# Half the Fourier rows from mirrored sums through DRAM, and a bank of the Fourier stage for every third MLP group

## The chip, the core and the metric

The kernel runs on one core of a Trainium2 chip. The core has a matrix engine (TensorE, "PE" in the profile, with "PEld" for its weight loads), a vector engine ("DVE"), a scalar engine ("ACT"), a general engine ("POOL") and a queue engine ("SP") that only issues transfers. Transfers go through 16 DMA engines, which the queues of SP, ACT and POOL share. The metric is the device time of one execution in microseconds; the lower the better. The kernel before takes 309.03 us, the median of 3 runs (308.47 to 309.29).

## The reference

Two parts run after each other. The first is attention by chunks: 4 batches, 8 heads, 768 positions of 64 elements. Chunks of 32 queries look at 16 positions to the left, their own 32, 8 to the right and 8 memory positions. The heads' outputs side by side give `x` of 4 x 768 x 512. The second part is a Fourier mixing layer with an MLP:

```python
X = np.fft.fft(x, axis=1)
X = np.fft.fft(X, axis=2)
mixed = np.real(X).astype(np.float32)
u = x + mixed
mu = np.mean(u, axis=-1, keepdims=True)
var = np.mean((u - mu) ** 2, axis=-1, keepdims=True)
un = (u - mu) / np.sqrt(var + 1e-06)
ch = np.maximum(un @ w_ch1, 0.0) @ w_ch2
return u + ch
```

Because `x` is real, `mixed[s, d]` equals `mixed[(768 - s) % 768, (512 - d) % 512]`: the rows 385 to 767 of `mixed` are the rows 383 to 1 with their columns mirrored.

## The kernel before

**Who sets the order.** Every piece of work is put on a list with `plan.add(engine, cost, emit, after, take, give, ...)`. `Plan.order` (line 62) plays the list through with these costs and returns one order of pieces; the kernel issues them in that order, and each engine executes its own part strictly in it. `take` and `give` are the buffers that a piece holds; a piece is placed when the plan believes its buffers free. Pieces marked `filler` (the MLP's matmuls) have the lowest rank on PE and are placed where nothing else is ready. Between engines the hardware waits on semaphores, whatever the plan believed.

**Stages of a batch.** Attention (`attention`, line 692) runs by pairs of heads, four pairs `n` a batch: loads of q and k on POOL's queue and of v on SP's (`e_load_v`, line 289, seven transfers for each pair), turns, scores, exponentials, values, and `e_norm` (line 376), which writes `xsb`, a tile of 128 partitions x 6 row tiles x 512. The Fourier stage (`first_fourier` for batch 0, `fourier` for the others) folds `xsb` on DVE, transforms along the sequence on PE (`e_rows`, line 433, into PSUM tiles `ps`), copies the result as two fp16 parts (`up`), reverses it for the upper half (`e_dn`, line 459), and transforms along the columns: `e_columns` (line 537) makes, for each of six row tiles `kt`, a PSUM tile `pm` with 8 matmuls of 128 columns of weights and 256 moving elements. `e_sum` adds `pm` to `xsb`, `e_stats` takes mean and variance, `e_un` subtracts the mean and casts, and `e_flip` (line 572) transposes the row tile with a transfer on SP, for batches 1 to 3; batch 0 does that on PE with `tp` tiles. The MLP of a batch (`mlp`, line 903) has two halves `sh` of three row tiles each: 16 groups `e_ch1` of four matmuls into `ph`, each followed by a relu on ACT (`e_relu`), then three row tiles `e_ch2` of 16 matmuls into `pc`, each followed by `e_osb` on DVE and a store `e_out` on ACT's queue.

**Banks of PSUM.** The tag "acc" has two banks for `ps` and `pm`, the tag "mlp" two for `ph`, `pc`, `tp`. Which one the MLP takes is said by

```python
def mtag(b, i):
    return "acc" if b == B - 1 and i % 3 == 2 else "mlp"
```

so only in the last batch does every third `ph` and `pc` go into an "acc" bank. The groups of `e_ch2` stand in a chain (`c2`, `mlp_prev`), so no later MLP group is placed before an earlier `e_ch2`.

**Transfers.** SP and ACT each issue their transfers in order. In the built program every transfer of these two queues takes the next of eight completion semaphores, in turn over both queues; it is issued only when the earlier transfer on that semaphore has completed. A transfer of one queue can thus wait for one of the other.

Of the kernel before, what the change touches and what calls it, by code (L numbers as in the profile page):

```python
# [10 lines left out]
FP32 = mybir.dt.float32  # L11
BF16 = mybir.dt.bfloat16
FP16 = mybir.dt.float16
AFT = mybir.ActivationFunctionType
ALU = mybir.AluOpType
# [16 lines left out]
def strided(src, off, dims):  # L32
    return bass.AP(tensor=src.tensor, offset=src.offset + off,
                   ap=[list(src.ap[0])] + [list(d) for d in dims])
# [105 lines left out]
def kernel(  # L140
# [11 lines left out]
    nc = tc.nc  # L152
    B, H, S, D = q.shape
    DM = out.shape[2]
# [35 lines left out]
    seq = [(b, pr) for b in range(B) for pr in (0, 2, 1, 3)]  # L190

    plan = Plan(dict(qs=NS, ks=NS, va=NV, kTb=NKT, qT=2, tr=1, sc=1, xa=1, e1=3,
                     xsb=3, fold=2, hl=1, up=4, dn=4, acc=2, mlp=2, un=6, unT=2, hT=1, osb=3))
    add = plan.add
    MLPS = 1000000

# [189 lines left out]
            xa[:, :, :, 0:D], zs.unsqueeze(3).to_broadcast([P, 3, 2, D]), ALU.mult)  # L386


    zy_of, pq_of, ff_of, hl_of, ps_of, up_of, pm_of, un_of, tp_of = ({} for _ in range(9))
    mu_of, unT_of, rstd_of, g_of = {}, {}, {}, {}  # L390
    mid = cpool.tile([P, 2, NST, 1], FP16)
    mid32 = cpool.tile([P, NST, 1], FP32)
    warm = cpool.tile([P, 1], FP32)
    gate = cpool.tile([P, 1], FP32)

    def e_zy(b, par, c):
# [60 lines left out]
                                up[:, 0].rearrange("p k s -> p s k"), ALU.subtract)  # L457

    def e_dn(b, par, ab):
        dn = fpool.tile([P, 2, HS], FP16, tag="dn", bufs=4, name="dn")  # L460
        nc.vector.tensor_copy(dn, rev_ap(up_of[b, par, ab][2], HS, HS, [[2 * NK, 2]]))
        up_of[b, par, ab][1] = dn

    def g_zy(par, g):
        if g == 0:
# [82 lines left out]

    def e_sum(b, kt):
        uv = xs[b][:, kt, :].rearrange("p (j c) -> p c j", c=2)  # L550
        nc.vector.tensor_tensor(uv, pm_of.pop((b, kt)), uv, ALU.add)  # L551

    def e_stats(b, kt):
        if kt == 0:
# [17 lines left out]
    def e_flip(b, kt):  # L572
        if kt == 0:
            unT_of[b] = fpool.tile([P, NDT, S], FP16, tag="unT", bufs=2, name="unT")
        nc.sync.dma_start_transpose(unT_of[b][:, :, ts(kt, P)], un_of.pop((b, kt)))

    def e_unT(b, kt):
        if kt == 0:
# [6 lines left out]
        nc.gpsimd.tensor_tensor(rstd, rstd, mhalf, ALU.pow)  # L585


    def mtag(b, i):
        return "acc" if b == B - 1 and i % 3 == 2 else "mlp"

    ph_of, pc_of, hT_of, osb_of = ({} for _ in range(4))

# [18 lines left out]
                             start=(ht == 0), stop=(ht == NHT - 1))  # L611

    def e_osb(b, sh, stl):
        st = sh * 3 + stl
        osb_of[b, st] = osb = fpool.tile([P, DM], FP32, tag="osb", bufs=3, name="osb")
        nc.vector.scalar_tensor_tensor(osb, pc_of.pop((b, sh, stl)), rstd_of[b][:, st:st + 1],  # L616
                                       xs[b][:, st, :], ALU.mult, ALU.add)

    def e_out(b, st):
        nc.scalar.dma_start(out[b, ts(st, P), :], osb_of.pop((b, st)))  # L620


    t_zero = add("DVE", 0.2, e_zero, rank=-21)
    t_table = add("ACT", 1.4, lambda: nc.scalar.activation(warm, zero, AFT.Sin), [t_zero], rank=-3)
# [169 lines left out]
    def first_fourier():  # L794
# [37 lines left out]
                                              give=(tag,))  # L832
        return columns_of(0, t_rest)

    def fourier(b):
        nrm = [[t_norm[b * HP + i, g] for i in ii for g in range(2)] for ii in ((0, 1), (2, 3))]
        t_rest = {}
        zy = {}
        ff = hi = None
        for par in range(2):  # L840
            zy[par] = [None]
            for c in range(2):
                zy[par].append(add("DVE", 0.96, lambda par=par, c=c: e_zy(b, par, c),
                                   nrm[c] + [ff, zy[par][-1]],
                                   take=("fold",) if c == 0 else ()))
            pq = add("DVE", 1.86, lambda par=par: e_pq(b, par), zy[par], take=("fold",),
                     give=("fold",))
            prev = pq
            for ab in range(2):
                ff = add("DVE", 1.1, lambda par=par, ab=ab: e_ff(b, par, ab), [pq, prev],  # L850
                         take=("fold",) if ab == 0 else (), give=("fold",) if ab == 1 else ())
                prev = ff
                hi = add("ACT", 0.85, lambda par=par, ab=ab: e_hi(b, par, ab), [ff, hi],
                         take=("hl",) if ab == 0 else ())
                lo = add("DVE", 0.96, lambda par=par, ab=ab: e_lo(b, par, ab), [hi],
                         give=("fold",) if ab == 1 else ())
                rw = add("PE", 1.95 if par == 0 and ab == 1 else 1.0,
                         lambda par=par, ab=ab: e_rows(b, par, ab), [lo, t_sines],
                         take=("acc",), give=("hl",) if ab == 1 else ())
                up = add("ACT", 0.6, lambda par=par, ab=ab: e_up(b, par, ab), [rw], take=("up",))  # L860
                t_rest[par, ab] = add("DVE", 0.6, lambda par=par, ab=ab: e_rest(b, par, ab),
                                      [up], give=("acc",))
        return columns_of(b, t_rest)

    def columns_of(b, t_rest):
        t_dn = {}
        for par in range(2):
            for ab in range(2):
                t_dn[par, ab] = add("DVE", 0.36, lambda par=par, ab=ab: e_dn(b, par, ab),
                                    [t_rest[par, ab]], take=("dn",))  # L870
        t_un = {}
        allr = list(t_rest.values())
        cols = {}

        def columns(kt):
            cols[kt] = add("PE", 0.9, lambda: e_columns(b, kt),
                           allr + [t_rows] + (list(t_dn.values()) if kt > 2 else []),
                           take=("acc",), rank=len(plan.tasks) + (15 if kt == 3 else 0),
                           give=("up",) * 4 if kt == 2 else ("dn",) * 4 if kt == 5 else ())

        sa = None
        columns(0)
        for kt in range(NST):
            if kt + 1 < NST:
                columns(kt + 1)
            su = add("DVE", 0.7, lambda kt=kt: e_sum(b, kt), [cols[kt]], give=("acc",))
            sa = add("DVE", 0.9, lambda kt=kt: e_stats(b, kt), [su, sa])
            un = add("ACT", 0.72, lambda kt=kt: e_un(b, kt), [sa], take=("un",))
            if b > 0:
                t_un[kt] = add("SP", 0.1, lambda kt=kt: e_flip(b, kt), [un, t_un.get(kt - 1)],  # L890
                               take=("unT",) if kt == 0 else (), give=("un",), moved=0.8,
                               loose=True)
                continue
            tp = add("PE", 0.26, lambda kt=kt: e_turn_u(b, kt), [un, t_idh], take=("mlp",),
                     give=("un",))
            t_un[kt] = add("DVE", 0.43, lambda kt=kt: e_unT(b, kt), [tp, t_un.get(kt - 1)],
                           take=("unT",) if kt == 0 else (), give=("mlp",))
        rs = add("POOL", 1.0, lambda: e_rstd(b), [sa])
        return t_un, rs
# [3 lines left out]
    def mlp(b, t_un, rs):  # L903
        for sh in range(2):
            relu = []
            c2 = None
            for ht in range(NHT):
                ph = add("PE", 0.65, lambda sh=sh, ht=ht: e_ch1(b, sh, ht),
                         mlp_prev + [t_un[3 * sh + i] for i in range(3)] + t_w1,
                         take=(mtag(b, ht),), give=("unT",) if sh == 1 and ht == NHT - 1 else (),  # L910
                         rank=MLPS + len(plan.tasks), filler=True)
                relu.append(add("ACT", 0.5, lambda sh=sh, ht=ht: e_relu(b, sh, ht),
                                [ph, relu[-1] if relu else None],
                                take=("hT",) if ht == 0 else (), give=(mtag(b, ht),),
                                rank=RELU(len(plan.tasks))))
            for stl in range(3):
                st = 3 * sh + stl
                for part in range(4):
                    end = part == 3
                    c2 = add("PE", 0.88, lambda sh=sh, stl=stl, part=part: e_ch2(b, sh, stl, part),  # L920
                             [relu[4 * part + 3], t_w2[part], c2], take=(mtag(b, stl),) if part == 0 else (),
                             give=("hT",) if stl == 2 and end else (),
                             rank=MLPS + len(plan.tasks), filler=True)
                os_ = add("DVE", 0.76, lambda sh=sh, stl=stl: e_osb(b, sh, stl), [c2, rs],
                          take=("osb",), 
                          give=(mtag(b, stl), "xsb") if st == NST - 1 else (mtag(b, stl),),
                          rank=RELU(len(plan.tasks)))
                mlp_prev[0] = c2
                add("ACT", 0.1, lambda st=st: e_out(b, st), [os_], give=("osb",), moved=0.9,
                    rank=RELU(len(plan.tasks)))  # L930

# [46 lines left out]
```

## Time and profile before

| | |
|---|---|
| median of 3 runs | 309.03 us (308.47 to 309.29) |
| the profiled execution | 308.85 us, of which 307.1 us are the span from first to last instruction |
| PE | 289.5 us busy (94%), 3148 matmuls |
| `ph` matmuls, L596 | 512, 91.6 us |
| `pc` matmuls, L610 | 384, 86.9 us |
| `pm` matmuls, L545 | 192, four groups of 48 with 9.2 us each |
| DVE, ACT, POOL | 171.2, 161.5, 40.8 us busy |
| DMA | 28.93 MB, mean 94 GB/s |

The profile is of one execution. A line "L545" is a line of the kernel; `out<-in` are tile names. Busy times of matmuls overlap, since they are pipelined, so their pace is better read from the chain of work that ended last, which is followed back from the last instruction, or from start to start in the order of time. Waits name the engine, the line and what ended the wait. Rows "SPq" are the queue's own: how long it stood at a transfer before issuing it, or took to issue it. The lines shown below are word for word from the profile and the answers of the trace.

### The profile page before, as it was taken

Reading aid. Unit: us, or ns where it says so; the run is one execution under the profiler, and the core shown is the slowest. Engines: PE = TensorE matmul, PEld = TensorE weight load, DVE = VectorE, ACT = ScalarE, POOL = GpSimd, SP = SyncE. Lnnn points to the kernel's source line nnn. Section 1 sums busy time; section 2 is a strip of 40 time slices with the busy share of each in tenths; the row PEclk is TensorE's granted clock in tenths of the full one; section 3 lists DMA queues with packets and bytes.
Section 4 is the critical chain, followed back from the end, with each engine's and each line's share of the span. In section 5 each row is a group of like instructions: output and inputs, shape, how many; then the busy total and the mean of one; then the engine's idle time right before and its main releaser. Section 6 shows DMA issues by size and latency. Waiting matters only on the chain.

```text
span 307.1 us, 7496 instructions
## 1 busy us (share of the span) xinstructions
PE 289.5 (94%) x3148; PEld 181.5 (59%) x3148; DVE 171.2 (56%) x371; ACT 161.5 (53%) x291; POOL 40.8 (13%) x78
## 2 busy tenths in 40 slices
PE   1399999999999999999989999999999999999994
PEld 1267678866666676666756646675554554554541
DVE  7877895975397887797764399476101001001001
ACT  6656373689884666885257423743360450531710
POOL 8806421132201102000020000000200000000000
PEclk9999999999999999999999999999999999999999
DMA  6989999999944925821361011004201101001011
GB/s 114 197 171 167 204 205 196 198 204 178 193 72 91 203 45 111 136 47 40 89 137 36 2 46 59 0 19 102 86 2 40 64 2 68 34 2 71 31 36 68
DMA packets 60289, 28.93 MB, mean 94 GB/s; under 512 B 48480, under 2 KB 56672, under 8 KB 60256
## 3 DMA queue, kind: packets, MB, share of 16 engines
q1 hardware_dynamic: 47168, 11.61, 21.0%
q0 software_dynamic: 9344, 10.49, 20.8%
q10 hardware_dynamic: 3744, 6.36, 5.7%
q8 instruction: 25, 0.41, 0.5%
q14 instruction: 8, 0.07, 0.1%
HBM read 30.28 MB, written 6.29 MB: 119 GB/s over the span
## 4 chain that ended last, share of the span: by engine, by line
PE 91%; DMA 2%; POOL 2%; DVE 1%; ACT 1%; issue 1%; POOLq 0%; ACTq 0%
PE ph L596 28%; PE pc L610 27%; PE xa L372 9%; PE pm L545 7%; PE ps L440 5%; PE idle L654 5%; PE ps L534 4%; PE sc L351 3%; DMA qs<-in_q_dram 2%; PE trk L313 2%; PE trq L313 2%; DVE osb L616 1%; POOL qs L286 0%; ACT hT L603 0%; PE tp L570 0%
## 5 line engine op out<-in xcount | busy, mean ns | idle before, releaser
L603 ACT ACTIVATE hT<-ph 128x384 f16<-128x384 f32 x128 | 60.9, 492 | 63.0 <-PE ph L596 51.5
L596 PE MATMUL ph<-unT,w_sb 128*128 128x384 f16 x512 | 91.6, 326 | 2.2 <-ACT hT L603 1.1
L610 PE MATMUL pc<-w_sb,hT 128*128 128x512 f16 x384 | 86.9, 379 | 0.0
L596 PEld LDWEIGHTS <-w_sb 128*128 128x128 f16 x512 | 47.8, 97 | 36.8 <-issue 5.7
L616 DVE SCALAR_TENSOR_TENSOR osb<-pc,rstd,xsb 128x512 f32<-128x512 f32 x24 | 18.0, 749 | 82.5 <-PE pc L610 82.4
L610 PEld LDWEIGHTS <-hT 128*128 128x128 f16 x384 | 36.8, 98 | 41.2 <-issue 0.2
L359 ACT ACTIVATE e<-sc,mbias 128x384 f32<-128x384 f32 x64 | 33.8, 583 | 13.8 <-PE sc L351 11.3
L372 PEld LDWEIGHTS xa<-va,e 128*64 128x64 f32 x768 | 25.0, 137 | 7.8 <-issue 7.0
L372 PE MATMUL xa<-va,e 128*64 128x65 f32 x768 | 29.3, 226 | 0.0
L563 ACT ACTIVATE un<-xsb,mu_s 128x512 f16<-128x512 f32 x24 | 17.2, 720 | 14.9 <-DVE mu_s L558 14.8
L382 DVE RECIPROCAL zs<-xa 128x6 f32<-128x6 f32 x32 | 6.1, 191 | 25.6 <-PE xa L372 25.5
L452 ACT CAST up<-ps 128x386 f16<-128x386 f32 x16 | 9.7, 603 | 19.1 <-PE ps L440 13.5
L551 DVE TENSOR_TENSOR xsb<-pm,xsb 128x512 f32<-128x512 f32 x24 | 16.0, 675 | 4.4 <-PE pm L545 4.2
L383 DVE TENSOR_TENSOR xsb<-xa,zs 128x384 f32<-128x384 f32 x32 | 17.8, 557 | 1.1
L557 DVE BATCH_NORM_STATS2 st<-xsb 128x6 f32<-128x512 f32 x24 | 16.4, 684 | 0.5
L654 PE MATMUL idle<-dz 128*128 128x384 bf16 x71 | 15.3, 350 | 1.0 <-DVE zero L230 1.0
L322 ACT COPY qT<-trq 128x768 bf16<-128x768 bf16 x16 | 12.8, 798 | 5.6 <-PE trq L313 5.5
L286 POOL DMA_DIRECT2D ks<-in_k_dram x16 | 10.2, 635 | 35.0 <-PE trk L313 31.4
L584 POOL TENSOR_SCALAR rstd<-mu_s 128x6 f32<-128x6 f32 x4 | 1.0, 245 | 102.0 <-DVE osb L616 57.7
L313 PE MATMUL trq<-ident_b,qs 96*64 96x96 bf16 x256 | 9.4, 221 | 5.1 <-DMA qs<-in_q_dram 5.1
L286 POOL DMA_DIRECT2D qs<-in_q_dram x16 | 10.5, 659 | 25.2 <-PE trq L313 21.5
L456 DVE TENSOR_TENSOR up<-ps,up 128x386 f16<-128x386 f32 x16 | 9.6, 598 | 7.5 <-ACT up L452 7.5
(126 smaller groups left out, 343.5 us busy)
## 6 DMA issues: line engine op xcount, KB each, us to landing
va<-in_v_dram SPq DMA_DIRECT2D x32, 220.0 KB
out_dram<-osb ACTq DMA_DIRECT2D x24, 256.0 KB
w_sb<-in_moe_w_ch_dram POOLq DMA_DIRECT2D x8, 512.0 KB, 16.9
qs<-in_q_dram POOLq DMA_DIRECT2D x16, 192.0 KB, 5.7
ks<-in_k_dram POOLq DMA_DIRECT2D x16, 192.0 KB, 6.1
va<-in_mem_v_dram SPq DMA_DIRECT2D x32, 24.0 KB
va<-in_v_dram SPq DMA_DIRECT2D x32, 22.0 KB
va<-in_v_dram SPq DMA_DIRECT2D x16, 32.0 KB
```

The costliest lines, as they stand in the source:

```text
L286: nc.gpsimd.dma_start(dst[n % NS][0:QP], src[b, 2 * pr:2 * pr + 2].rearrange("h (p j) d -> p h (j d)", j=RB))
L313: nc.tensor.transpose(out_[64 * hh:64 * hh + 64, j * w:(j + 1) * w], src[:, hh, j * D:(j + 1) * D], eye)
L359: nc.scalar.activation(e1[:, :, :, ts(half, 32)], sc[:, :, 0:6, ts(half, 32)], AFT.Exp, bias=mbias[:, half:half + 1], scale=1.0 / math.sqr ...
L372: nc.tensor.matmul(xa[64 * half:64 * half + 64, st, hh, 0:65], e1[:, hh, t6, :], v1[:, hh, 6 * g + t6, 0:65], start=True, stop=True)
L383: nc.vector.tensor_tensor(xs[b][:, 3 * g:3 * g + 3, 2 * pr * D:(2 * pr + 2) * D] .rearrange("p s (h d) -> p s h d", h=2), xa[:, :, :, 0:D] ...
L545: nc.tensor.matmul(pm[:, par, :], lhs, rhs[:, par, :], start=(im == 0), stop=(im == 3))
L563: nc.scalar.activation(un, xs[b][:, kt, :], AFT.Identity, bias=mu_of[b][:, kt, 0:1], scale=-1.0)
L596: nc.tensor.matmul(ph[:, 0:384], w1_sb[:, dt, ts(ht, P)], unT_of[b][:, dt, sh * 384:(sh + 1) * 384], start=(dt == 0), stop=(dt == NDT - 1))
L603: nc.scalar.activation(hT_of[b, sh][:, ht, :], ph_of.pop((b, sh, ht))[:, 0:384], AFT.Relu, bias=0.0, scale=-1.0)
L610: nc.tensor.matmul(pc_of[b, sh, stl], hT_of[b, sh][:, ht, ts(stl, P)], w2_sb[:, ht, :], start=(ht == 0), stop=(ht == NHT - 1))
L616: nc.vector.scalar_tensor_tensor(osb, pc_of.pop((b, sh, stl)), rstd_of[b][:, st:st + 1], xs[b][:, st, :], ALU.mult, ALU.add)
L654: nc.tensor.matmul(fill_of[0][:, 0:384], dz, strided(dz, 0, [[0, 3], [1, P]]), start=True, stop=True)
```

## The change

Two things change. First, in batches 1 to 3 `e_columns` makes only the row tiles 0, 1 and 2, the rows 0 to 383. The other three are gained from the same PSUM tiles: `e_back` writes the three upper row tiles of `xsb` to a DRAM tensor with their rows backwards inside blocks of 64, `e_mirror` reads them back into `xr` so that partition p of tile t holds row 768 - (128 t + p), and `e_sum_back` adds `pm`, read with its columns backwards, to `xr` and writes the sum into the upper half of `xsb`. Row 384, which has no mirror image, is made by `e_last_row` in row 0 of the first `pm`, after `e_sum` has read it. A `pm` bank is therefore held until `e_sum_back` has read it. The row tiles of these batches are worked on in the order 0, 3, 1 ... (`kts`, `SLOT`), and the outputs of the mirrored ones go to a second DRAM tensor (`e_out_rows`, on SP) and from there backwards to the output (`e_out_back`, on SP). `dn`, needed for batch 0 alone, becomes one buffer, which `xr` shares. Second, `mtag` gives the "acc" bank to every third MLP group in all batches.

In the built program SP issues 42 transfers more, nine of `e_back`, twelve each of `e_mirror` and `e_out_back` and nine of `e_out_rows`, and ACT nine stores less. The first `e_back` stands between the loads of v for pairs 11 and 12, its `e_mirror` between the loads for pairs 12 and 13; those of batch 2 stand behind the last load. Before `e_back` of batch 1, load 11 stands on the semaphore of batch 0's store of row tile 2. The third `e_mirror` transfer of batch 3 stands on that of batch 1's store of row tile 1.

```diff
     def e_dn(b, par, ab):
-        dn = fpool.tile([P, 2, HS], FP16, tag="dn", bufs=4, name="dn")
+        if b not in dn_of:
+            dn_of[b] = fpool.tile([P, 4, 2, HS], FP16, tag="dn", bufs=1, name="dn")
+        dn = dn_of[b][:, 2 * par + ab]
...
+    xd = nc.dram_tensor("x_rows", [2, 3, P, DM], FP32).ap()
+    od = nc.dram_tensor("out_rows", [2, 3, P, DM], FP32).ap()
...
+    def e_back(b):
+        for t in range(3):
+            r0 = xd[b % 2, t, 63:64, :]
+            nc.sync.dma_start(bass.AP(tensor=r0.tensor, offset=r0.offset,
+                                      ap=[[64 * DM, 2], [-DM, 64], [1, DM]]), xs[b][:, 5 - t, :])
+
+    def e_mirror(b):
+        xr_of[b] = xr = fpool.tile([P, 3, DM], FP32, tag="dn", bufs=1, name="xr")
+        xb = xd[b % 2].rearrange("t p d -> p t d")
+        nc.sync.dma_start(xr[1:65], xb[64:128])
+        nc.sync.dma_start(xr[65:128], xb[0:63])
+        nc.sync.dma_start(xr[0:1, 1:3], xb[63:64, 0:2])
+        nc.sync.dma_start(xr[0:1, 0:1], xb[63:64, 2:3])
+
+    def e_last_row(b):
+        pm = pm_of[b, 0]
+        for par in range(2):
+            todo = [(up_of[b, par, ab][0][:, part, HS:HS + 1], (cosD, nsinD)[ab])
+                    for ab in range(2 - par) for part in range(2)]
+            for i, (lhs, rhs) in enumerate(todo):
+                nc.tensor.matmul(pm[0:1, par, :], lhs, rhs[:, par, :], start=(i == 0),
+                                 stop=(i == len(todo) - 1))
+
+    def e_sum_back(b, kt):
+        pm, xr = pm_of.pop((b, kt)), xr_of[b]
+        y = xs[b][:, 3 + kt, :].rearrange("p (j c) -> p c j", c=2)
+        r = xr[:, kt, :].rearrange("p (j c) -> p c j", c=2)
+        nc.vector.tensor_tensor(y[:, :, 1:HD], strided(pm, HD - 1, [[HD - 1, 2], [-1, HD - 1]]),
+                                r[:, :, 1:HD], ALU.add)
+        nc.vector.tensor_tensor(y[:, :, 0], strided(pm, 0, [[2 * HD - 1, 2]]), r[:, :, 0],
+                                ALU.add)
...
+    SLOT = (0, 3, 4, 5, 1, 2)
...
     def mtag(b, i):
-        return "acc" if b == B - 1 and i % 3 == 2 else "mlp"
+        return "acc" if i % 3 == 2 else "mlp"
...
+    def e_out_rows(b, st):
+        nc.sync.dma_start(od[b % 2, st - 3], osb_of.pop((b, st)))
+
+    def e_out_back(b, st):
+        t = st - 3
+        p0 = 1 if t == 0 else 0
+        src, r0 = od[b % 2, t, p0:P, :], S - P * t - p0
+        top = out[b, r0:r0 + 1, :] if r0 < S else out[b, 0:1, :]
+        half = [[1, HD]]
+        nc.sync.dma_start(bass.AP(tensor=top.tensor, offset=top.offset,
+                                  ap=[[HD, 2], [-DM, P - p0]] + half),
+                          bass.AP(tensor=src.tensor, offset=src.offset,
+                                  ap=[[HD, 2], [DM, P - p0]] + half))
+        if p0:
+            nc.sync.dma_start(out[b, HS:HS + 1, :], od[b % 2, 0, 0:1, :])
...
     def fourier(b):
+        t_x1 = add("SP", 0.4, lambda: e_back(b), [t_norm[b * HP + i, 1] for i in range(HP)],
+                   moved=2.0, loose=True)
+        t_xr[b] = add("SP", 0.4, lambda: e_mirror(b), [t_x1], take=("dn",), moved=2.0, loose=True)
...
+        else:
+            kts = (0, 1, 3, 4, 2, 5)
...
+            if b > 0 and kt > 2:
+                if kt == 3:
+                    cols[kt] = add("PE", 0.7, lambda: e_last_row(b), [t_sum[0]])
+                return
...
+            if b == 0 or kt < 3:
+                su = add("DVE", 0.7, lambda kt=kt: e_sum(b, kt), [cols[kt]],
+                         give=("acc",) if b == 0 else ())
+                t_sum[kt] = su
+                if b > 0 and kt == 0:
+                    columns(3)
+            else:
+                su = add("DVE", 0.8, lambda kt=kt: e_sum_back(b, kt - 3),
+                         [cols.get(kt), t_sum[kt - 3], t_xr[b]],
+                         give=("acc", "dn") if kt == 5 else ("acc",))
...
+                if b and st > 2:
+                    o1 = add("SP", 0.1, lambda st=st: e_out_rows(b, st), [os_], give=("osb",),
+                             moved=0.9, loose=True)
+                    add("SP", 0.1, lambda st=st: e_out_back(b, st), [o1], moved=0.9, loose=True)
+                    continue
```

## The prediction

> **What bounds the kernel now.** I read the page's busy shares, its 40 slices, the chain that ended last, then the shapes, stretches, waits and order of time where the change acts.
>
> ```profile
> PE 289.5 (94%) x3148; PEld 181.5 (59%) x3148; DVE 171.2 (56%) x371; ACT 161.5 (53%) x291; POOL 40.8 (13%) x78
> ...
> PE   1399999999999999999989999999999999999994
> ...
> DMA  6989999999944925821361011004201101001011
> ...
> q1 hardware_dynamic: 47168, 11.61, 21.0%
> ...
> PE 91%; DMA 2%; POOL 2%; DVE 1%; ACT 1%; issue 1%; POOLq 0%; ACTq 0%
> ```
>
> PE is full from about 20 us to 303 us and is 91% of the chain. So PE work that goes is time gained, and every us in which PE, which works in program order, stands still is time lost. The other engines and the DMA engines have room after 85 us. Two stretches of the same work, the MLP of batch 2 and that of batch 3, differ only in that batch 3 puts every third group into "acc":
>
> ```profile
> 217.80:261.30 43.50, 43.12 (x225) 21.72 (x224) 4.50 (x6) 15.71 (x32) 1.59 (x2) 1.00 0.10 37
> 261.30:303.10 41.80, 41.80 (x225) 21.83 (x223) 4.50 (x6) 14.62 (x32) 0.00 (x0) 1.00 0.10 38
> ```
>
> The second figure is the stretch in us. The order of time of the chain gives the pace on PE: 16 column matmuls in 1.75 us, so 0.109 each. It also shows matmuls at half pace after PE had waited 7 us (338 ns each, later 180):
>
> ```profile
> 8.86 7.01 DMA qs<-in_q_dram
> ...
> 16.77 2.03 PE idle L654 x6
> ...
> 24.89 0.92 PE idle L654 x5
> ...
> 157.06 0.50 ACT hT L603
> ...
> 158.84 0.71 ACT un L563
> ...
> 201.72 1.75 PE pm L545 x16
> ```
>
> On SP, the waits by total and two rows in order of time (start, length):
>
> ```profile
> SPq L295 <- DMA out_dram<-osb: 31.0, 3, 13.2
> ```
> ```profile
> 82.84 0.88 SPq L295 DMA_DIRECT2D va<-in_v_dram  x2
> 95.36 0.27 SPq L304 DMA_DIRECT2D va<-in_mem_v_dram  x1
> ```
>
> SP stood from 83.7 to 95.4 us in the middle of a load of v, for an *output store of ACT*: it is on the same one of the eight completion semaphores. Its `osb` began at 92.3 us and took 0.75, so a store is seen as landed 2.3 us after its `osb`. Today nobody waits for that load. What the change puts behind it on SP, somebody will.
>
> **The change part by part.**
>
> *Less PE work.* 3 batches x 3 column tiles x 8 matmuls = 72 x 0.109 = 7.9 us go. `e_last_row` adds 3 x 6 matmuls with one column of weights and 256 moving elements. The one-column matmuls of L440 (245 to 247 ns) last as long as its full ones (245 to 248), so 18 x 0.109 = 2.0 us. Net **-5.9**.
>
> *A bank more for the MLP of batches 0 to 2.* For batch 2: 43.50 - 41.80 = **-1.7**. Before 217.8 us the groups of four `ph` matmuls take 4.6 us more, start to start, than 0.65 us each: 1.75 in four stalls (the rows at 157 and 158.8 us end two, a relu and what stood before it on ACT), the rest in steps of 0.09. Ends: 0 and -4.6; I take **-3.0**, since the steps are the same as batch 2's, which all go, but ACT is busier here (79.4 of 117.6 us). A 0.8 us stall of the `tp` transposes at 70 us, for a "mlp" bank, goes too: **-0.7**. Twelve `dn` copies (12 x 0.36 us of DVE) go and nine two-column adds (0.17, as L416) come; DVE is covered by PE except in the next three parts.
>
> *"acc" held from `columns` to `e_sum_back`, batch 3.* The planned order there is columns 0, columns 1, last row, columns 2, then `e_ch2` of a third tile, which now wants "acc" too; no filler lies between, since the MLP groups follow each other. From the start of columns 0: the first `e_sum` starts at 1.08 (201.55 to 202.63 us in the trace), sum and stats step by 1.53, so the first `e_sum_back` starts at 4.2. It takes 0.68 + 0.17 (a reversed read costs nothing: 947 ns for 762 elements in L417, 954 for 768 forward in L407). Columns 2 can start at 5.1; PE is there at 0.87 + 0.87 + 0.65 = 2.4: 2.7 lost. The next release is 1.75 later, at 6.85, columns 2 ends at 6.0: 0.9 more. Also, the third mirror transfer of batch 3 waits on SP for the semaphore of batch 1's store of row tile 1, whose product ends as columns 0 begins: 0.3 + 0.75 + 2.3, two issues of 0.3, 1.5 to land, 5.5 instead of 4.2. I add 1.4: **+5.0** (3.6 to 8). Batches 1 and 2 have fillers in these places.
>
> *The rows through DRAM, batch 1.* The price is that of `e_back`. The nearest rows are the stores of `osb`: 128 packets of 2 KB, 84 ns apart on one DMA engine, 8 on each of 16 engines, 0.7 us. But their outermost dimension is 128; that of `e_back`'s destination is 2 (two blocks of 64 rows backwards). The trace tells how many engines a copy uses: each closes with a four-byte packet. Of q1's 47,168 packets, 45,312 carry 256 bytes (16 loads of v at 2,256, 18 flips at 512). The other 1,856 are 16 x 80 + 18 x 32, and 80 for the seven copies of a load is 16 for each of the three with 64 or 80 rows and 8 for each of the four with 8 rows. So the outermost count sets the number of engines. Ends: 16 engines, 0.7 us for each of the three copies, and 2 engines, 64 x 84 ns = 5.4 us each, 16.2 us on the same two engines. I take 2, as the 8-row copies are nearest.
>
> The Trainium skill, "DMA: Bandwidth & Descriptors", section "Why a DMA increments its semaphore by 16 and not by 1", says that a hardware-generated copy runs on the largest number up to 16 that divides the outermost sizes of both sides. By this page `e_back` (2 and 128) runs on 2 engines, as I took; no transfer of this trace has an outermost 2.
>
> Zero is the end of batch 0's third `e_ch2` tile. On PE come 8 `ch1`, 2 `rows`, 3 `values`, 2 `scores`, 2 turns, 2 `columns` and the last row: columns 2 of batch 1 is reached at 14.3. On SP, load 11 waits for that tile's store: about 0.5 + 0.75 + 2.3, with DVE's queue 3.8. Two issues (0.7) and one more: `e_back` runs from 5.0 to 21.2, and lands at 22.6 (1.4, the store's 2.3 less issue and data). Load 12 is issued between and has 164 packets of 22 ns on those two engines: 3.6. The mirror's 33 packets of 86 ns: 2.8; landing 1.4: 29.0. `e_sum_back` 0.85: columns 2 starts at 29.9, not 14.3: **+15.6**. With 16 engines the rows are there at 12.5, DVE wants them at 13.3: 0. With POOL's loads sharing the two engines it is up to 20.
>
> *Batch 2.* Zero is the end of batch 0's last tile. `e_back` is issued at 0.8 after load 15 (2 us of packets): 2.8 + 16.2 + 1.4 = 20.4, mirror 0.5 + 2.8 + 1.4: 25.1, released at 26.0. PE is at columns 2 at 23.1: **+2.9** (0 to 7). In batch 3 the same path ends together with the store's semaphore above and adds nothing.
>
> *PE after 15 us of standing still.* By the first rows about 4 us at half pace: **+2.0** (0 to 4).
>
> *The outputs of half the rows* go out in two transfers on SP. No engine waits for the second; the last such tile is two tiles (2 x 3.46 us) from the end, so the tail from the last `osb` (303.15 us) stays. Flips and loads that move behind them have 10 us and more. ACT issues nine stores fewer. Nothing.
>
> Sum: -5.9 - 1.7 - 3.0 - 0.7 + 5.0 + 15.6 + 2.9 + 2.0 = **+14.2**. The profiled execution took 308.85 us (span 307.1 and 1.75 around it), which gives 323.05; the median, 309.03, is 0.18 above: **323.2 us**.
>
> **The rivals.**
>
> *The copies are spread and the rows are in time.* The DMA engines are at 0.36 to 0.96 around batch 1 and 768 KB take 2.1 us over 16 of them. Against it: the 8-row copies. -11.3 + 5.0 = -6.3: 302.7 (300 to 306). It ends on the other side; the point is a round trip of batch 1 under some 8.5 us from `e_back`'s issue to the mirror's landing, against 24 here. Breaking even needs the three batches together to wait 11.3 us.
>
> *The banks stop PE in every batch, with the copies spread.* If DVE runs later than planned, columns 2 of batches 1 and 2 wait as in batch 3: 3 x 5.0 - 11.3 = +3.7: 312.7. Against it: three `ch1`, 1.95 us, lie before columns 2 in both.
>
> *Part of the way.* The two-engine copies start earlier or DVE's adds come later, so that batch 1 waits 5 to 8 us: 308 to 312.
>
> **How the numbers follow.** A change under 0.3% (0.9 us) cannot be told from none here. Likeliest case 0.70, own range 313 to 333 (gains 7.6 to 13, waits 16 to 34, not all at one end); spread copies 0.20; banks in every batch 0.05; part of the way 0.05. The range leaves out the lower quarter of the spread case and the top of the first: 302 to 332. Faster: 0.20. Same: 0.02, from the fourth. Slower: 0.78.
>
> **What would show it.** In the changed profile DVE's longest wait is `e_sum_back` on `xr` in batch 1, 15 us, and PE's is `e_columns` behind it: a hole of some 15 us in PE's slices at 105 to 130 us, a smaller one in batch 2, 4 to 6 us before batch 3's columns 2. `e_back`'s packets lie on two engines: few GB/s for 16 us. Column matmuls fall from 192 to 138, and the MLP of batch 2 takes 41.8 us. If there is no hole in batch 1, the engine count was wrong and 302.7 is nearer. If columns 2 waits with `xr` long landed, it is the banks.

## The result and the profile after

The changed kernel takes 338.64 us, the median of 4 runs (335.41 to 342.77), beside 309.16 us for the kernel before (308.47 to 309.58). The ratio is 1.086 (95% interval 1.082 to 1.090). Two of the four runs took some 5 us longer than the other two; medians here and below are of all runs, ratios leave such longer runs out. The profiled execution took 336.03 us (span 334.3), 27.2 us more than that of the kernel before. The direction was right, and 302 to 332 us was too low.

The page of the kernel after, the same rows as were shown before, and the granted clock:

```profile
PE 287.8 (86%) x3094; PEld 178.5 (53%) x3094; DVE 168.3 (50%) x368; ACT 163.1 (49%) x291; POOL 40.7 (12%) x78
...
PE   1599999999999900799999699997699999999990
...
PEclk9999999999999975599999899999599999999997
DMA  7989999999473336747611632124293212102121
...
q1 hardware_dynamic: 53282, 21.05, 30.0%
...
PE 74%; DMA 14%; SPq 5%; POOL 2%; DVE 1%; ACT 1%; issue 1%; DVEq 0%; POOLq 0%; ACTq 0%
```

The column matmuls that are gone show in the count (54 fewer in all: 72 less, 18 more). PE now has three dips, at the slices from 117, 184 and 226 us, and an empty last slice, and behind each dip the clock is low. DMA and SP's queue, 2% of the chain before, are 19%, and SP's queue (q1) moves 21.05 MB instead of 11.61. The waits of PE, then those of DVE (us in total, times, longest):

```profile
PE pm L581 <- DVE xsb L497: 27.7, 3, 18.8
```
```profile
DVE xsb L495 <- DMA xr<-x_rows: 26.7, 3, 19.6
...
DVE osb L657 <- DMA out_dram<-osb: 6.6, 1, 6.6
```

All three holes are `e_columns` waiting for `e_sum_back`, which waits for `xr`: the case that the forecast held likeliest, in its three places. The last row is new: DVE's final `osb` waits for a store. The chain in order of time (start, length), around batches 1 and 3 and at the end:

```profile
118.50 3.35 SPq L295
...
127.58 0.61 SPq L477
...
129.48 5.39 DMA xr<-x_rows
134.99 0.69 DVE xsb L495
135.81 1.89 PE pm L581 x8
...
229.11 0.76 DVE osb L657
229.89 3.87 DMA out_dram<-osb
233.78 0.65 SPq L479
234.47 1.76 DMA xr<-x_rows
236.36 0.69 DVE xsb L495
237.17 1.89 PE pm L581 x8
...
323.20 0.76 DVE osb L657
323.98 6.49 DMA out_dram<-osb
330.59 0.75 DVE osb L657
```

Eight column matmuls take 1.89 us after a hole, against 0.87. Two rows in order of time on SP belong to them:

```profile
106.39 4.95 SPq L471 DMA_DIRECT2D x_rows<-xsb  x3
...
127.58 0.61 SPq L477 DMA_DIRECT2D xr<-x_rows  x1
```

The copies of batch 1 were issued at 106.4 us, their readback (L477) at 127.6. Between lie 384 packets of 2 KB, the first at 107.6 and the last at 126.6 us: 19.0 us, which at 93 ns a packet is the work of two DMA engines. Three stretches of windows (bounds; length, PE busy, PEld, DVE, ACT, POOL; clock; DMA share; GB/s) show the half pace and the MLP of batches 2 and 3:

```profile
130.00:140.00 10.00, 4.20 (x49) 3.19 (x50) 4.80 (x12) 1.45 (x2) 0.00 (x0) 0.50 0.83 148
```
```profile
243.32:284.95 41.63, 41.63 (x226) 21.93 (x225) 4.50 (x6) 15.37 (x33) 1.59 (x2) 1.00 0.40 77
284.95:326.60 41.65, 41.65 (x225) 21.82 (x223) 4.50 (x6) 15.71 (x32) 0.00 (x0) 1.00 0.16 58
```

The two MLPs are now equal, as forecast. Laid out from start to start on PE, the profiled executions differ so:

| term | forecast | measured |
|---|---|---|
| hole in batch 1 | +15.6 | +19.0 |
| hole in batch 2 | +2.9 | +3.4 |
| hole in batch 3 | +5.0 | +5.8 |
| PE at half pace behind them | +2.0 | +6.2 (2.9, 1.4, 1.8) |
| end: last `osb` 3.9 us after its product | 0 | +3.9 |
| `ph` before 217.8 us, MLP of batch 2, `tp` | -5.4 | -5.6 |
| column matmuls | -5.9 | -5.6 (not from this trace: r18 to r19 below) |
| sum | +14.2 | +27.1, against 27.2 |

### The profile page after: what moved, and what is told of

It reads as the page before. It is cut to its first block, busy times and chain, and to the rows that moved or that the text cites. A ratio compares the mean times of both kernels' runs of the same rounds, so it can differ in the third digit from the quotient of the medians.

```text
span 334.3 us, 7430 instructions
## 1 busy us (share of the span) xinstructions
PE 287.8 (86%) x3094; PEld 178.5 (53%) x3094; DVE 168.3 (50%) x368; ACT 163.1 (49%) x291; POOL 40.7 (12%) x78
## 3 DMA queue, kind: packets, MB, share of 16 engines
q1 hardware_dynamic: 53282, 21.05, 30.0%
q0 software_dynamic: 9344, 10.49, 19.7%
## 4 chain that ended last, share of the span: by engine, by line
PE 74%; DMA 14%; SPq 5%; POOL 2%; DVE 1%; ACT 1%; issue 1%; DVEq 0%; POOLq 0%; ACTq 0%
PE pc L651 24%; PE ph L637 22%; PE xa L372 7%; DMA x_rows<-xsb 4%; DMA out_dram<-osb 4%; PE idle L710 4%; PE pm L581 4%; DMA xr<-x_rows 4%; PE ps L570 3%; PE ps L442 3%; PE sc L351 2%; DMA qs<-in_q_dram 2%; SPq L295 2%; PE trq L313 2%; PE trk L313 2%
## 5 line engine op out<-in xcount | busy, mean ns | idle before, releaser
L637 PE MATMUL ph<-unT,w_sb 128*128 128x384 f16 x512 | 89.8, 328 | 0.0
L651 PE MATMUL pc<-w_sb,hT 128*128 128x512 f16 x384 | 88.4, 384 | 0.0
L637 PEld LDWEIGHTS <-w_sb 128*128 128x128 f16 x512 | 48.5, 98 | 32.9 <-issue 1.3
L359 ACT ACTIVATE e<-sc,mbias 128x384 f32<-128x384 f32 x64 | 33.7, 579 | 18.9 <-PE sc L351 18.8
L581 PE MATMUL pm<-cosD,up 128*128 128x256 f16 x48 | 10.6, 309 | 27.7 <-DVE xsb L497 27.7
L372 PE MATMUL xa<-va,e 128*64 128x65 f32 x768 | 30.0, 229 | 0.0
L581 PEld LDWEIGHTS <-up 128*128 128x128 f16 x96 | 9.8, 108 | 31.2 <-DVE xsb L497 28.8
L495 DVE TENSOR_TENSOR xsb<-pm,xr 128x510 f32<-128x510 f32 x9 | 6.1, 673 | 26.7 <-DMA xr<-x_rows 26.7
```

What stands on the lines that cost most here:

```text
L359: nc.scalar.activation(e1[:, :, :, ts(half, 32)], sc[:, :, 0:6, ts(half, 32)], AFT.Exp, bias=mbias[:, half:half + 1], scale=1.0 / math.sqr ...
L372: nc.tensor.matmul(xa[64 * half:64 * half + 64, st, hh, 0:65], e1[:, hh, t6, :], v1[:, hh, 6 * g + t6, 0:65], start=True, stop=True)
L581: nc.tensor.matmul(pm[:, par, :], lhs, rhs[:, par, :], start=(im == 0), stop=(im == 3))
L637: nc.tensor.matmul(ph[:, 0:384], w1_sb[:, dt, ts(ht, P)], unT_of[b][:, dt, sh * 384:(sh + 1) * 384], start=(dt == 0), stop=(dt == NDT - 1))
L651: nc.tensor.matmul(pc_of[b, sh, stl], hT_of[b, sh][:, ht, ts(stl, P)], w2_sb[:, ht, :], start=(ht == 0), stop=(ht == NHT - 1))
```

## The experiments

### One part alone

r1 is the changed kernel with the copy in forward order, so that its outermost size is 128; it leaves the reversal out:

```diff
-            r0 = xd[b % 2, t, 63:64, :]
-            nc.sync.dma_start(bass.AP(tensor=r0.tensor, offset=r0.offset,
-                                      ap=[[64 * DM, 2], [-DM, 64], [1, DM]]), xs[b][:, 5 - t, :])
+            nc.sync.dma_start(xd[b % 2, t], xs[b][:, 5 - t, :])
```

> The three copies of the upper row tiles go to DRAM with their rows in forward order (outermost size 128 instead of 2), nothing else differs: the reversal is left out, so the rows 385 to 767 of batches 1 to 3 are gained from the wrong rows. Theory A (the copy runs on two DMA engines because its outermost size is 2): the packets of the three copies take 2 to 3 us instead of 19, PE's hole in batch 1 falls from 19.0 us plus 2.9 at half pace to under 4 in all, the one in batch 2 from 3.4 to 0, batch 3 keeps 4 to 6 us and the tail is as it was: 309 to 314 us. Theory B (the place on SP: the readback stands behind a load of v whose transfers wait for semaphores of stores, whatever the copy takes): batch 1 still waits 8 to 12 us, 321 to 328 us. Theory C (the banks): columns 2 waits about 3 us in each batch with the rows long landed, 316 to 319 us.

r1: 317.11 us (ratio to before 1.024, 1.018 to 1.030). In order of time on SP, in its page, and in its chain:

```profile
108.06 2.00 SPq L470 DMA_DIRECT2D x_rows<-xsb  x3
```
```profile
q1 hardware_dynamic: 53408, 21.05, 31.9%
```
```profile
113.59 0.57 SPq L475
...
115.48 6.84 DMA xr<-x_rows
122.44 0.69 DVE xsb L493
123.25 1.89 PE pm L579 x8
```

The 384 packets lie between 108.9 and 111.5 us: 2.6 us instead of 19.0, with 85 ns a packet. SP's queue moves the same 21.05 MB in 126 packets more (53,408 against 53,282): the sizes of the data packets are the same, and the 126 are four-byte closing packets, 14 more for each of the nine copies, as for 16 engines instead of 2. So the outermost size did set the number of DMA engines. Batch 1's hole falls from 19.0 to 4.6 us, batch 2's to none, batch 3's to 3.7: theory A, 3 us above its range. What is left in batch 1 is the readback: issued only after load 12, and 6.8 us long, in which its packets took 144 ns each beside the next loads.

r2 does the same on the way out, for the row tiles 4 and 5, and leaves their reversal out:

```diff
     def e_out_back(b, st):
...
+        if t:
+            nc.sync.dma_start(out[b, r0 - P + 1:r0 + 1, :], src)
+            return
```

> Of the transfers that bring the mirrored outputs from DRAM to the output, those of the row tiles 4 and 5 write their rows in forward order (outermost size 128 instead of 2): the reversal of these rows is left out, nothing else differs. Theory A (the last row tile waits because the store whose buffer it reuses has an eighth of its packets behind a two-engine transfer): the store lands some 2.3 to 2.8 us after it was issued instead of 6.5, the last osb starts when its product is done, at 3.5 to 4 us earlier: 332 us. Theory B (one buffer alone is free for the last three tiles, and a store takes about 4 us in any case, as it does at 230 us): 335 to 336 us, as before.

r2: 333.62 us (1.080, 1.075 to 1.085). The last three `osb` of r2:

```profile
321.22 0.75 DVE L657 SCALAR_TENSOR_TENSOR osb<-pc,rstd,xsb 128x512 f32<-128x512 f32 x1 [13.10 <-PE pc L651]
324.67 0.75 DVE L657 SCALAR_TENSOR_TENSOR osb<-pc,rstd,xsb 128x512 f32<-128x512 f32 x1 [2.70 <-PE pc L651]
328.13 0.75 DVE L657 SCALAR_TENSOR_TENSOR osb<-pc,rstd,xsb 128x512 f32<-128x512 f32 x1 [2.71 <-PE pc L651]
```

The last waits for its product alone, and the span ends 3.8 us later, at 331.9. That is theory A in mechanism; the whole is not quite 3.9 us less because batch 3's hole was 7.2 us this time. In the changed kernel the last `osb` got the buffer of the tile before, whose store went out at 323.98. Of its 128 packets 112 had run by 325.6, and the other 16 began at 328.65, behind a two-engine transfer of `e_out_back` issued at 322.57. The end is thus the same two engines once more.

r3 is the kernel before with the new `mtag`, r4 the changed kernel with the old one:

```diff
-        return "acc" if b == B - 1 and i % 3 == 2 else "mlp"
+        return "acc" if i % 3 == 2 else "mlp"
```

> The kernel before with only the bank of every third MLP group changed. Theory A (the terms of the prediction): MLP of batch 2 from 43.5 to 41.8 us, the other ph groups 3.0 us less (0 to 4.6), the turns at 70 us 0.7 less: -5.4, about 303.5 us (302 to 307). Theory B (the MLP groups hold banks that the Fourier stages of batches 1 to 3 want, which then wait for relus and osb): 309 us or more.

r3: 310.95 us (1.005, 1.003 to 1.008; 309.46 in the profiled run), so theory A's time is wrong. Its terms are there: the `ph` groups lose 4.5 us from start to start, `tp` 0.8. But PE has a wait that the kernel before does not have:

```profile
PE ph L596 <- DMA unT<-un: 3.7, 1, 3.7
```

It lasts from 144.7 to 148.4 us, with some 1.6 us lost to half pace after it (1.2 in the `ps` matmuls, 0.4 in `ph`): PE reaches the MLP of batch 1 before that batch's flips have come. Neither theory had named this: the time lies in B's range, but PE waits for none of B's banks.

> The changed kernel with the bank of every third MLP group as it was before (only in the last batch). Theory A (the bank's gain of 5.4 us adds to the rest): 336.0 + 5.4 = 341 us (338 to 343). Theory B (the gain lies where PE waits for the mirrored rows anyway): 335 to 337 us.

r4: 359.79 us (1.163, 1.161 to 1.166). Neither theory holds: with the old bank rule the changed kernel is 24 us slower (than 335.4 and 336.0), not 5. The holes are 22.1 us in batch 1, 17.2 in batch 2 (3.4 with the banks) and 4.8 at 256 us, where `ph` waits for an `osb`. In batch 2 SP reaches the copies at 167.3 us and PE is done with its last group before columns 2 at 177.0, against 164.3 and 186.7 in the changed kernel: with the other bank rule the order leaves 13 us less between the two, so more of the same slow copy shows. The two parts of the change are not additive.

### The path of the rows, and the end

r5 issues `e_back` on POOL's queue, and the planner is told so:

```diff
-            nc.sync.dma_start(bass.AP(tensor=r0.tensor, offset=r0.offset,
+            nc.gpsimd.dma_start(bass.AP(tensor=r0.tensor, offset=r0.offset,
...
-        t_x1 = add("SP", 0.4, lambda: e_back(b), [t_norm[b * HP + i, 1] for i in range(HP)],
-                   moved=2.0, loose=True)
+        t_x1 = add("POOL", 3.0, lambda: e_back(b), [t_norm[b * HP + i, 1] for i in range(HP)],
+                   moved=5.4)
```

> The three copies of each batch's upper row tiles to DRAM are issued on POOL's queue instead of SP's, with the same two blocks of 64 reversed rows. Theory A1 (two engines for each copy, but POOL's queue gives each copy a pair of its own and does not stand behind load 11): the copies are issued some 15 us earlier and take 5.5 to 8 us together, PE's hole in batch 1 falls from 19.0 us to under 4, batch 2's to 0: 308 to 313 us. Theory A2 (the same two engines for all three on this queue too): issued earlier but 16 to 19 us long, hole 2 to 6 us: 312 to 320 us. Theory B (the readback's place on SP decides, not the copy): hole of 10 us or more remains, above 324 us.

r5: 316.18 us (1.022, 1.015 to 1.029). Batch 1's hole is 4.3 us, batch 2 has none. The page's row of the copies (KB each, median us from issue to landing) says why:

```profile
x_rows<-xsb POOLq DMA_DIRECT2D x9, 256.0 KB, 12.4
```

The time and the hole are in A2's range. The three copies of a batch still take 11 to 13 us from first to last packet, between what A1 and A2 expected; but batch 1's are issued at 86.9 us instead of 106.4, since POOL does not stand behind load 11. The hole that is left is again the readback on SP, issued at 112.8. r1 and r5 come to the same time, one by a shorter copy, the other by an earlier one.

r6 stays on SP and copies three quarters of the columns a pair of heads earlier (`e_back(b, last)`, placed after three and after four pairs):

```diff
+        c0, c1 = (6 * D, DM) if last else (0, 6 * D)
...
-                                      ap=[[64 * DM, 2], [-DM, 64], [1, DM]]), xs[b][:, 5 - t, :])
+                                      ap=[[64 * DM, 2], [-DM, 64], [1, c1 - c0]]),
+                             xs[b][:, 5 - t, c0:c1])
```

> On SP as in the changed kernel, but three quarters of the columns are copied when the third pair of heads is normalised and the last quarter (512-byte packets, about 30 ns each by 22 ns for 256 and 46 for 1,024 bytes) after the fourth; the plan is told longer landings. Theory A (two engines, 16 to 19 us of packets on the path): only 3 x 64 x 30 ns = 5.8 us stay behind the last pair: hole in batch 1 19.0 - 11 = 6 to 10 us, batch 2 none: 318 to 324 us. Theory B (place on SP): three more transfers on SP put the readback no earlier: 334 us or more.

r6: 343.66 us (1.108, 1.101 to 1.114): theory A missed. In order of time on SP:

```profile
94.59 12.22 SPq L472 DMA_DIRECT2D x_rows<-xsb  x3
...
113.98 2.83 SPq L472 DMA_DIRECT2D x_rows<-xsb  x3
```

The early part stood 12 us on SP, most of it for the semaphore of a store, and the late part came at 114.0, 7.6 us later than the whole copy before. The readback still went out at 122.9 us instead of 127.6, and batch 1's hole is 13.3 us instead of 19.0, above A's 6 to 10. The time is in theory B's range, though not for B's reason: PE now waits 7.4 us for flips, and 8.3 us in batch 3. The shorter last part helped batch 1; the changed order cost more elsewhere.

r8 changes only what the planner believes:

```diff
-                   moved=2.0, loose=True)
-        t_xr[b] = add("SP", 0.4, lambda: e_mirror(b), [t_x1], take=("dn",), moved=2.0, loose=True)
+                   moved=2.0, late=15.0, loose=True)
+        t_xr[b] = add("SP", 0.4, lambda: e_mirror(b), [t_x1], take=("dn",), moved=2.0, late=2.5, loose=True)
```

> Only the planner's belief changes: it is told that the copy lands 15 us later and the readback 2.5 us later than it thought; the transfers are the same. It then places columns 2 of batch 1 some 6 us later behind MLP groups, but also the readback later on SP. Theory A (the hole is late rows, whose cover can be planned): hole of batch 1 12 to 15 us: 327 to 332 us. Theory B (SP's order decides): the readback goes behind another load of v and the hole stays or grows: 335 us or more.

r8: 340.79 us (1.099, 1.095 to 1.104). The time is theory B's: the planner moved columns 2 some six us back, but also the readback behind another load of v. In the profile that went out at 136.6 us instead of 127.6, and PE still waited 18.5 us. The profile is of its longest run (347.56 us), so the hole of the others is not shown.

r9 leaves the copies as they are and changes three other things:

```diff
-    SLOT = (0, 3, 4, 5, 1, 2)
+    SLOT = (3, 4, 5, 0, 1, 2)
...
-        half = [[1, HD]]
+        part = [[1, DM // 16]]
...
-                                  ap=[[HD, 2], [-DM, P - p0]] + half),
+                                  ap=[[DM // 16, 16], [-DM, P - p0]] + part),
...
+    def ptag(b, kt):
+        return ("xa", "tr", "sc")[kt] if b == B - 1 else "acc"
```

> The changed kernel with three things outside the copies altered: the mirrored row tiles are the first half of each batch's MLP instead of lying in its middle, the transfers that bring them to the output have sixteen pieces of 128 bytes of a row as outermost size instead of two, and in the last batch the pm tiles take the banks of attention, so that nothing waits for them. Theory A: the tail's 3.9 us and batch 3's 5.8 + 1.8 us go, the holes of batches 1 and 2 stay: 336.0 - 11.5 = 324.5 us (322 to 328). Theory B (the last tiles wait for a buffer in any case; batch 3's MLP waits for the late row tiles instead): 331 us or more.

r9: 327.51 us (1.060, 1.054 to 1.067). Theory A within its range: batch 3 has no hole and the last `osb` waits for its product. Batch 1 keeps 19.1 us; batch 2 loses its hole, but PE waits 3.8 us for flips at 162 us. The rows still run backwards on their way out, now in sixteen pieces: the packets of most tiles take 1.5 to 1.8 us (3.2 in one) instead of 5.5 to 7.4. So the reversal is not what made such a transfer slow.

### The next wait, and what it hides

r10 is r5 and r9 together, with the planner told that the readback lands 2.5 us later. r12 takes everything new off SP: copy, readback and way out on POOL's queue, the stores of mirrored `osb` on ACT's. r13 is r12 with r6's two parts. The core of r12:

```diff
-        nc.sync.dma_start(xr[1:65], xb[64:128])
+        nc.gpsimd.dma_start(xr[1:65], xb[64:128])
...
-        nc.sync.dma_start(od[b % 2, st - 3], osb_of.pop((b, st)))
+        nc.scalar.dma_start(od[b % 2, st - 3], osb_of.pop((b, st)))
...
-        nc.sync.dma_start(bass.AP(tensor=top.tensor, offset=top.offset,
+        nc.gpsimd.dma_start(bass.AP(tensor=top.tensor, offset=top.offset,
```

> The copies of the upper row tiles on POOL's queue, as in r5, together with the three alterations of r9 (mirrored tiles in the first half of the MLP, sixteen pieces as outermost size on the way out, pm of the last batch in the banks of attention). If the two sets act in different places, as the holes say (r5: batch 1 4.3 us and batch 2 none; r9: batch 3 and tail), the sum is 316.2 - 2.6 (batch 3) - 1.8 (relu behind a store at 265 us) - 3.9 (tail) = 308 us (305 to 311). If the time that PE gains is met by the next late transfer (the flips of batch 1 at 145 to 165 us, as in r3, r6 and r9): 311 to 316 us.

> As r10, but none of the new transfers stands on SP: copy, readback and the way out on POOL's queue, the stores of the mirrored osb on ACT's like the others. Theory B (the rest of batch 1's hole is SP's order: the readback waits behind loads of v that wait for stores): hole of batch 1 under 1.5 us, flips no later than in the kernel before: 300 to 306 us. Theory D (POOL then holds back the loads of q and k, or its transfers run on few engines): new waits of PE at trq or trk, 308 us or more.

> As r12, with the copy in two parts, three quarters of the columns after the third pair of heads, the rest after the fourth. On POOL's queue, where nothing waits for stores, the rows are in DRAM some 8 us earlier than in r12: if the copy's length is what is left of the hole, 1 to 3 us faster than r12; if POOL's issues (three more a batch) are on the way of the q and k loads, slower than r12.

r10: 318.50 us (1.027), r12: 326.33 (1.053), r13: 323.12 (1.044). All three expectations missed: r10 lies above both of its ranges, r12 far above theory B's without theory D's waits, and r13's gain of 3.2 us on r12 has another source than the one named. In r12 and r13 no PE wait for `xr` of over 0.2 us is left, and yet they are slower than r10. Most of the time sits in one place, the flips of batch 1 (9.6 us in r10, 23.5 in r12, 19.7 in r13). In r13, the waits of PE and of SP's queue, and SP and ACT in order of time:

```profile
PE ph L643 <- DMA unT<-un: 19.7, 1, 19.7
```
```profile
SPq L304 <- DMA out_dram<-osb: 24.0, 2, 22.2
```
```profile
112.87 2.49 SPq L295 DMA_DIRECT2D va<-in_v_dram  x2
137.56 0.27 SPq L304 DMA_DIRECT2D va<-in_mem_v_dram  x1
...
140.62 2.60 SPq L617 DMA_TRANSPOSE unT<-un  x2
```
```profile
129.04 0.34 ACTq L667 DMA_DIRECT2D out_dram<-osb  x1
```

SP stands from 115.4 to 137.6 us inside a load of v. In the built program this transfer has the completion semaphore of the store that ACT issues at 129.04, whose packets ran until 137, beside the copies of batch 2. The flips are behind it. It is the wait that the prediction read from the kernel before (SP from 83.7 to 95.4 us), only that now PE comes early enough to feel it. r14 puts all stores of `osb` on POOL's queue, off these eight semaphores; r15 does that for r3, r16 for the kernel before.

```diff
-        nc.scalar.dma_start(out[b, ts(st, P), :], osb_of.pop((b, st)))
+        nc.gpsimd.dma_start(out[b, ts(st, P), :], osb_of.pop((b, st)))
```

> As r13, with all stores of osb on POOL's queue too, so that SP and ACT's semaphores carry only loads of v and flips. Theory B (a flip waits because a load of v before it on SP waits for the semaphore of a store whose product PE has yet to make): the 19.8 us wait for unT goes, and with it nothing is left of the new waits: 321.8 - 20 = 300 to 304 us. Theory E (the flips are late because PE reaches the MLP of batch 1 before their row tiles are summed; the order of the work, not the semaphores): a wait of 10 us or more stays, 312 us or more.

> The kernel before with the bank of every third MLP group changed (r3) and all output stores on POOL's queue. Theory B: r3's wait of 3.8 us for unT and 1.1 at half pace after it go: 310.0 - 5 = 304 us (302 to 306). Theory E: as r3, 308 to 312 us.

> The kernel before with all output stores on POOL's queue, nothing else. PE waits for none of SP's transfers there after 42 us, so nothing to gain: 308 to 311 us, with 1 us more at the end if a store from POOL lands later.

r14: 306.31 us (0.987, 0.982 to 0.992). r15: 307.76 (0.994, 0.992 to 0.997). r16: 312.64 (1.009, 1.006 to 1.013). The wait for flips falls from 19.7 to 2.2 us in r14 and is gone in r15: theory B's mechanism. But r14 and r15 lie 2.3 and 1.8 us above the ranges expected for it, and r16 0.6 above its own with the 1 us allowed for the end. The move itself costs 3 us, nearly all at the end: r16's last `osb` starts at 303.40 us as before, and its span ends 7.7 us later instead of 4.0. Against r16 the banks alone bring 4.9 us, where the forecast had 5.4.

r17 and r18 are r14 and r15 with the last batch's unmirrored stores back on ACT. r19 is r17 with the mirrored tiles first in the last batch only:

```diff
-        nc.gpsimd.dma_start(out[b, ts(st, P), :], osb_of.pop((b, st)))
+        (nc.scalar if b == B - 1 else nc.gpsimd).dma_start(out[b, ts(st, P), :], osb_of.pop((b, st)))
...
-    SLOT = (3, 4, 5, 0, 1, 2)
+    SLOT = {1: (0, 3, 4, 5, 1, 2), 2: (0, 3, 4, 5, 1, 2), 3: (3, 4, 5, 0, 1, 2)}
```

> As r14, with the stores of the last batch's unmirrored tiles back on ACT's queue, where no load or flip is behind them. The end after the last osb goes from 5.1 to about 4.0 us: r14's 306.3 less 1 us: 303 to 306 us. If the sums are worth their 5.9 us of PE work, 2 to 4 us less than r18.

> As r15 (the kernel before, the banks, stores on POOL's queue), with the stores of the last batch back on ACT's queue. The end after the last osb goes from 7.7 to 4.0 us: 307.8 - 3.7 = 304 us (303 to 305.5). The forecast's terms for the banks alone give 309.0 - 5.4 = 303.6. If r17 is no lower than this, the mirrored sums bring nothing on this chip that the banks do not bring alone.

> As r17, but only the last batch has its mirrored tiles in the first half of the MLP; batches 1 and 2 have the changed kernel's order (0, 3, 4, then 5, 1, 2), so that the first half of batch 1 needs the flips of three early row tiles and not the last one behind the load of v for the last pair. If that wait (5.3 us and 1.9 at half pace in r17's profiled execution) hides the gain of the sums: 299 to 301.5 us, 3 to 5 us less than r18, and with less scatter than r17. If the sums bring nothing beside the banks: 303 to 306 us.

r17: 306.27 us (six runs from 301.36 to 308.06). r18: 304.25 us (0.984, 0.980 to 0.987), its expected time. r17's best run is below what was expected, the others at its upper end or above: in the longest, the profiled one, PE waited 5.1 us for the last flip of batch 1, which r9's order had made a condition of that batch's first MLP group. With r17 no lower than r18, r18's test said that the sums bring nothing beside the banks; r19 takes that wait away. r19: **298.61 us** (297.85 to 299.17; 0.965, 0.962 to 0.968), 0.4 us below its range and the fastest of all kernels here, 10.7 us below the kernel before. Its page:

```profile
PE 282.1 (95%) x3094; PEld 176.3 (59%) x3094; DVE 168.5 (57%) x368; ACT 162.2 (55%) x291; POOL 86.3 (29%) x141
...
PE   1399999999999999999999999999999999999994
...
PEclk9999999999999999999999999999999999999999
```

After the first 42 us PE has no wait of over 0.2 us. Between r18 and r19 lie the mirrored sums without their waits: 304.25 - 298.61 = 5.6 us. From start to start the `pm` matmuls take 5.7 us less on PE (16.1 instead of 21.8).

## Why the prediction was wrong

The path that the prediction followed was right. Two steps failed: the outputs were put at nothing and cost 3.9 us, and the half pace was counted for one hole at +2.0 and cost 6.2 over three. Batch 1's way through DRAM was put 3.4 us too short.

- **The mechanism of batch 1** (two engines, readback behind load 12, columns 2 behind `xr`) was right, and r1 shows it by the size alone. The term was 3.4 us too small: the copies took 19.0 us instead of 3 x 5.4 = 16.2, at 93 ns a packet and not 84 (batch 2's: 15.4 us, at 84), and from their last packet to the readback's landing it was 8.3 us (126.6 to 134.9) instead of 7.8.
- **Batch 2** (+2.9; measured 3.4) was right for these copies; r4 shows how much of it hung on the order.
- **Batch 3**: the semaphore of batch 1's store was named, and the chain shows it (L479 after the store at 229.89). The banks alone would have cost 2.6 us (`e_sum_back` could have begun at 233.1, PE stood from 231.4), the store 3.2 more; it landed 4.7 us after its `osb` began, where the prediction had 2.3.
- **Half pace was mis-sized**, the largest miss: +2.0 for batch 1 alone, measured 6.2 over three holes. The shorter holes cost 1.4 and 1.8 us.
- **"The outputs ... Nothing" was wrong**: 3.9 us. The prediction asked which engine waits for the second transfer, and none does; it did not ask which other transfer shares its two engines, nor which buffer the last `osb` would get.
- **The gains were right**: column matmuls -5.6 (-5.9), banks -5.6 in the changed kernel and -4.9 against r16 (-5.4). r19's 298.6 us lies 0.9 above 309.0 less the four gains, and 4.1 below the rival with spread copies, which had kept batch 3's 5.0.
- **The rivals**: the banks in every batch did not appear, since `xr` came last each time. The spread copies give 317.1 us in r1, not 302.7: the readback's 4.6 us, the half pace and the end were missing there too.
- The misses of 3.4, 0.5, 0.8, 4.2 and 3.9 us add up to 12.8, nearly all of 13.0 between forecast and profiled execution. All point one way, where the forecast's range had been drawn with "not all at one end".

The Trainium skill, "DMA: Bandwidth & Descriptors", section "Why a DMA increments its semaphore by 16 and not by 1", gives two engines for these copies; r1 agrees (19.0 and 2.6 us). Its page "TensorE: Matmul & The Clock Gate", Part 1, puts the array's clock at half after an idle window of about 3.4 us, and back after a busy one. The trace agrees (0.50 granted from 130 to 140 us). By that page each hole of 3.4 us or more costs an estimated 1.7 us afterwards (half of 3.4), 5.1 for three; measured were 6.2.

What stays open: why r5's copies, on POOL's queue, take 11 to 13 us; and why a store on POOL's queue ends the span 7.7 us after the last `osb` in r15 and r16 but 5.1 in r14.

## What to carry to other kernels

When a change adds a transfer, count three things besides its bytes: on how many DMA engines its outermost size puts it, which transfers of *other* queues then sit behind it on these engines, and whose completion semaphore it inherits. Price each wait of a full PE of some 3 us or more with the half pace behind it, and look at every buffer that waits for a store at the end. A gain that does not show (r3) may only have run into the next late transfer: move that, and measure again.

## What the runs showed of the hardware

- A store issued on ACT's queue had the packets of two of its sixteen DMA engines delayed by 3.1 us (325.5 to 328.65) behind a transfer of SP's queue, though the queues differ; after that the two alternated packet by packet.
- Readbacks from DRAM took 120 to 128 ns for a packet of 2 KB in the changed kernel and 111 to 144 in r1, by batch, against 84 to 93 for the copies to it.
- The same copies on POOL's queue (r5) went in packets of 4 KB, with means of 215 to 249 ns by batch.
- After 42 us, PE's waits of 3.2 us (batch 2 of the changed kernel) to 23.5 us (r12) were all followed by a granted clock of 0.5; that of 3.0 us in r2 was not, one of 2.75 us in r8 was. The low stretches lasted 3.41 us or a whole multiple of it: 6.83 us at the hole of 5.6 us, 20.48 at that of 18.8.
